# Transposes of three more tiles moved from TensorE to DMA in a chunked-attention and gated-FFN kernel, with later loads, other planned landing times and 12 load buffers

## The chip, the cores and the metric

The kernel runs on one core of a Trainium2 chip. The metric is the device time of one execution in microseconds (us). Three runs of the kernel before gave 244.65, 244.76 and 244.78 us.

## What is computed

An attention over chunks of 32 rows is followed by a gated feed-forward network (FFN). There are 4 batches, 8 heads, 768 rows and a head dimension of 64; each chunk sees 16 rows to its left, itself, 8 rows to its right, and 8 memory rows of its head.

```
for c in range(nc):                       # 24 chunks of 32 rows, batch and head by batch and head
    k_full = concat(mem_k, k[c*32-16 : c*32+40]);  v_full likewise
    a = softmax(q[c] @ k_full.T / 8);     out[c] = a @ v_full
x = out, as 3072 rows of 512
y = (maximum(x @ w_gate, 0) * (x @ w_val)) @ w_out      # 512 -> 1536 -> 512
```

Inputs and output are float32 in HBM; inside, the matmuls run on 16-bit tiles.

## The kernel before

The 3072 rows are 24 tiles of 128, six to a batch (tiles 0 to 5 are batch 0, 6 to 11 batch 1, 12 to 17 batch 2, 18 to 23 batch 3). The FFN works on blocks of tiles: `BLOCKS = [2, 2, 2, 4, 4, 4, 4, 2]`, so block 3 is tiles 6 to 9, block 4 tiles 10 to 13, block 5 tiles 14 to 17.

*A tile's attention.* q and k come in as `qk_b` (a load by POOL's queue that casts to bf16, line 254) and are transposed to `qT` and `kT`; `scores` (line 309) writes S to PSUM; DVE and ACT make the softmax `p_n` (lines 322 to 352); P is transposed to `pT`; `values` (line 388, or 374 and 381 in batch 0) multiplies by `v_bd`, and `x_copy` puts the result, already transposed, into the block's `xT`. The scores of a tile need the k of the next tile of its batch too. `v_bd` holds v of one batch in the layout that the values need; there are two of them, used in turn, so batch 2's v goes where batch 0's was (after the values of tile 5 and after zeroing, lines 134 and 136), and batch 3's where batch 1's was (after the values of tile 11). v comes by four loads of POOL (line 185) and eight copies of the memory rows (line 168); `upper` (from line 190) shifts rows inside it.

*Two ways to transpose.* For tiles below `LATE_QK` (q, k) and `LATE_P` (P), PE does it: four 128x128 products with an identity (line 275 for q and k, 358 for P; 236 in batch 0), and ACT or DVE copies the result out of PSUM. For tiles from that number on, a transposing DMA from SP's queue does it (line 283 for q and k, line 362 for P). q and P land where they are used; k lands in `k_t` (three buffers) and is copied into `kT` by DVE or ACT.

*A block's FFN.* For each of 12 column groups, `first` (line 407) makes `g_ps` and `v_ps` with four matmuls each, ACT applies the relu (line 413), DVE multiplies (line 419); then `second` (line 432) makes the outputs, which ACT copies and sends out from its own queue (line 439).

*What sets the order.* Nothing is ordered by hand. Each piece of work is an `op` with its engine, an assumed duration, the work that it depends on, a priority and the buffers that it takes and gives. `schedule()` (line 682) walks through assumed time and, on each engine, starts the ready op of best priority: attention has priority 1, FFN 2, so that FFN fills PE between the attention's steps. A dependency may carry a lag, as `(("t", a, 0), LAND)`: the transfer counts as landed that long after its issue. On PE, after an assumed 36 us, attention ops also wait for a `MARGIN` of 1.0 us. The order so found is the order of instructions in each engine's queue; at run time each queue goes strictly in that order and waits for what its next instruction really needs. POOL's loads go in the order of the list built from line 639 on: `late` is k and q of tiles 6 to 23, in that order (k, q, k, q), and slices of it are put behind each batch's v (line 674).

*Holding back.* `pace(a)` keeps PE's transposes of tile a from being planned before the FFN has reached a point that lies `LEAD` = 31 us of assumed FFN time ahead of the tile's block, plus `STEP` = 5.2 us per tile within the block. It is used only for tiles that PE transposes. `pace_t(a)` keeps the transposing transfers of tile a behind the scores of tile a - 6.

## Time and profile before

| | |
|---|---|
| median of three runs | 244.76 us |
| the profiled execution's own time | 244.74 us |
| its span in the trace | 242.7 us |
| PE busy, matmuls | 235.8 us, 2706 |
| DVE, ACT, POOL busy | 147.9, 136.0, 77.9 us |
| granted TensorE clock | 0.998 |
| bytes by DMA, mean rate | 25.17 MB, 104 GB/s |
| transposing transfers of SP | 9 of k, 9 of q, 9 of P |

The page cuts the span into 40 slices of about 6 us and gives each engine's busy share in tenths. Instructions are named by line: L407 is line 407. A row of the chain has a start, a length and what ran; it goes from the last instruction back to whatever released each step. A row of a timeline has a start, a length, the engine, the line, the operation, the tile written and the tile read, and in brackets the idle time before it. SPq and POOLq are the queues from which DMAs are issued. A queue's row gives packets, MB, and the time of its packets as a share of 16 engines; several packets can be in flight on one engine, so a share may pass 100%. q0 carries POOL's loads, q1 SP's transfers, q10 the outputs.

Landmarks, from PE's timeline: scores of tile 12 at 101.35 us, of 13 at 109.90, of 14 at 126.17; values of tile 11 at 105.51, of 12 at 111.02, of 13 at 118.12, of 14 at 136.84, of 17 at 150.63, of 18 at 154.60; first matmul of block 3 at 85.66, of block 4 at 122.40, of block 5 at 160.12. POOL's last loads for tile 23 are issued at 122.45.

### The profile page before, as it was taken

The page shows a single profiled execution, that of the slowest core. Times are in us where ns is not written, and L with a number is a line of the kernel's source. Part 1 is how long each engine was busy: PE and PEld are TensorE (multiplying, and loading weights), DVE is VectorE, ACT ScalarE, POOL GpSimd, SP SyncE. Part 2 cuts the span into 40 slices and gives each one's busy share as a digit, 9 for nine tenths or more (in the row PEclk, how much of TensorE's full clock was granted, in tenths as well). Part 3 has the DMA queues.
Part 4 walks back from the last instruction along what each step waited for, and adds up shares of the span by engine and source line. Part 5 has one row for each costly group of instructions (what it writes and reads, how often), then busy time and mean ns, then how long its engine had stood idle before and what let it go on. Part 6 is the DMA issues. An engine that isn't in the chain of part 4 may idle for free.

```text
span 242.7 us, 6546 instructions
## 1 busy us (share of the span) xinstructions
PE 235.8 (97%) x2706; PEld 140.8 (58%) x2706; DVE 147.9 (61%) x296; ACT 136.0 (56%) x288; POOL 77.9 (32%) x102
## 2 busy tenths in 40 slices
PE   7898999999999999999999999999999999999994
PEld 5587887884589545554544545554445444445873
DVE  6674876988877458977549999894431043410430
ACT  7477777767885499665756674453332233312432
POOL 8975689235984396037430000000000000000000
PEclk9999999999999999999999999999999999999999
DMA  6999999999999999999990142651001210012102
GB/s 72 172 179 203 201 164 172 193 131 134 191 195 154 80 168 136 120 124 153 116 218 7 36 53 48 131 133 24 0 0 46 86 43 0 3 43 86 43 3 86
DMA packets 96413, 25.17 MB, mean 104 GB/s; under 512 B 87424, under 2 KB 93312, under 8 KB 96384
## 3 DMA queue, kind: packets, MB, share of 16 engines
q0 software_dynamic: 76128, 14.65, 83.5%
q1 hardware_dynamic: 16656, 3.82, 15.0%
q10 hardware_dynamic: 3600, 6.29, 8.1%
q8 instruction: 21, 0.34, 0.7%
q14 instruction: 8, 0.07, 0.1%
HBM read 28.55 MB, written 6.29 MB: 144 GB/s over the span
## 4 chain that ended last, share of the span: by engine, by line
PE 88%; ACT 4%; DMA 2%; POOL 2%; DVE 2%; issue 1%; ACTq 0%; POOLq 0%
PE v_ps L407 26%; PE g_ps L407 25%; PE out_ps L432 22%; PE xT_ps L388 3%; DMA v_n<-in_v_dram 2%; PE s_ps L309 2%; PE idle_ps L141 2%; PE vs_ps L215 2%; PE xT_ps L381 2%; PE pT_ps L358 2%; ACT v_bd L79 1%; PE qk_ps L275 1%; PE qk_ps L236 1%; POOL qk_p L227 1%; ACT o_sb L79 1%
## 5 line engine op out<-in xcount | busy, mean ns | idle before, releaser
L419 DVE TENSOR_TENSOR gvT<-v_ps,g_relu 128x256 f16<-128x256 f32 (+1 forms) x96 | 52.9, 554 | 58.2 <-PE v_ps L407 43.2
L407 PE MATMUL v_ps<-xT,w_val_sb 128*128 128x256 f16 (+1 forms) x384 | 78.2, 326 | 0.1
L407 PE MATMUL g_ps<-xT,w_gate_sb 128*128 128x256 f16 (+1 forms) x384 | 78.2, 326 | 0.0
L413 ACT ACTIVATE g_relu<-g_ps 128x256 f16<-128x256 f32 (+1 forms) x96 | 47.0, 491 | 47.6 <-PE g_ps L407 45.9
L432 PE MATMUL out_ps<-w_out_sb,gvT 128*128 128x512 f16 (+2 forms) x300 | 65.3, 371 | 0.0
L407 PEld LDWEIGHTS <-w_gate_sb 128*128 128x128 f16 x384 | 36.3, 98 | 23.1
L407 PEld LDWEIGHTS <-w_val_sb 128*128 128x128 f16 x384 | 36.0, 98 | 22.3 <-issue 0.5
L432 PEld LDWEIGHTS <-gvT 128*128 128x128 f16 x300 | 27.9, 98 | 29.9
L79 ACT COPY o_sb<-out_ps 128x512 f32<-128x512 f32 (+2 forms) x25 | 14.2, 567 | 31.8 <-PE out_ps L432 25.6
L337 ACT ACTIVATE p_exp<-dif 128x256 f16<-128x256 f32 (+2 forms) x72 | 19.6, 340 | 4.4 <-DVE dif L329 3.5
L322 DVE TENSOR_REDUCE mx<-s_ps 128x8 f32<-128x512 f32 x24 | 16.5, 688 | 5.6 <-PE s_ps L309 5.4
L341 DVE TENSOR_REDUCE sm<-p_exp 128x8 f32<-128x512 f16 x24 | 16.4, 683 | 4.4 <-ACT p_exp L337 4.1
L254 POOL DMA_DIRECT2D qk_b<-in_q_dram x18 | 16.4, 912 | 7.4 <-DMA v_bd<-in_v_dram 5.5
L254 POOL DMA_DIRECT2D qk_b<-in_k_dram x18 | 16.2, 903 | 5.5 <-DMA w_out_sb<-in_moe_w_out_dram 4.4
L79 ACT COPY v_bd<-v_bd 24x768 f16<-24x768 f16 (+1 forms) x20 | 15.6, 818 | 2.2 <-ACT o_sb L79 1.2
L352 DVE TENSOR_TENSOR p_n<-p_exp,rinv 128x512 f16<-128x512 f16 x24 | 16.5, 687 | 0.4
L329 DVE TENSOR_TENSOR dif<-s_ps,mx 128x512 f32<-128x512 f32 x24 | 16.4, 682 | 0.2
L185 POOL DMA_DIRECT2D v_bd<-in_v_dram x12 | 10.9, 920 | 12.5 <-PE v_ps L407 11.8
L168 POOL DMA_DIRECT2D v_bd<-vmem x16 | 10.5, 661 | 12.5 <-DMA v_bd<-in_v_dram 10.5
L79 ACT CAST xT<-xT_ps 128x512 f16<-128x512 f32 x17 | 9.9, 583 | 6.2 <-PE xT_ps L388 4.8
L141 PE MATMUL idle_ps<-idle 128*128 128x256 bf16 x69 | 11.5, 319 | 1.1 <-DVE warm L475 1.1
L388 PEld LDWEIGHTS <-v_bd 128*128 128x128 f16 x288 | 9.7, 96 | 3.2 <-issue 0.2
(57 smaller groups left out, 179.5 us busy)
## 6 DMA issues: line engine op xcount, KB each, us to landing
out_dram<-o_sb ACTq DMA_DIRECT2D x23, 256.0 KB
qk_b<-in_k_dram POOLq DMA_DIRECT2D x18, 128.0 KB, 7.2
qk_b<-in_q_dram POOLq DMA_DIRECT2D x18, 128.0 KB, 7.0
v_bd<-in_v_dram POOLq DMA_DIRECT2D x6, 384.0 KB, 11.5
w_out_sb<-in_moe_w_out_dram POOLq DMA_DIRECT2D x2, 768.0 KB, 10.5
qk_p<-in_k_dram POOLq DMA_DIRECT2D x3, 256.0 KB, 5.7
qk_p<-in_q_dram POOLq DMA_DIRECT2D x3, 256.0 KB, 6.6
v_n<-in_v_dram POOLq DMA_DIRECT2D x6, 128.0 KB, 6.5
```

What stands on the lines that cost most here:

```text
L79: nc.scalar.copy(o, i)
L254: nc.gpsimd.dma_start(qk_b[a, i], bass.AP(tensor=x.tensor, offset=x[b, 0, 128 * t, 0].offset, ap=[[D, 128], [S * D, H], [1, D]]))
L322: nc.vector.reduce_max(SM[a, "mx"], s4, axis=AX.X)
L329: nc.vector.tensor_tensor(out=SM[a, "dif"].rearrange("p (m r) a s -> p r m a s", r=2), in0=S_ps.pop(a).rearrange("p r (m a) s -> p r m a s ...
L337: nc.scalar.activation(p[:, :, :, s0:s0 + k1 - k0], dif[:, :, :, k0:k1], ACT.Exp, scale=SCALE)
L341: nc.vector.reduce_sum(SM[a, "sm"], SM[a, "p"], axis=AX.X)
L352: nc.vector.tensor_tensor(out=P_n[a], in0=SM.pop((a, "p")), in1=rinv_b, op=ALU.mult)
L388: nc.tensor.matmul(ps[:, hp, r], lhsT=v_bd[b % NSET][:, hp, 4 * t + g, :], rhs=x[:, hp, r], start=True, stop=True)
L407: nc.tensor.matmul(ps, lhsT=w[:, f, 128 * m:128 * m + 128], rhs=xTs[blk][:, f, :], start=(f == 0), stop=(f == NFC - 1))
L413: nc.scalar.activation(st["r", m], st.pop((0, m)), ACT.Relu)
L419: nc.vector.tensor_tensor(out=st["gv"][:, m, :], in0=st.pop((1, m)), in1=st.pop(("r", m)), op=ALU.mult)
L432: nc.tensor.matmul(st["o", t, c], lhsT=st["gv"][:, m, 128 * t:128 * t + 128], rhs=w_out_sb[:, m, c[0]:c[1]], start=(m == 0), stop=(m == ND ...
```

## The change

- `LATE_QK` and `LATE_P` go from 15 to 12: tiles 12, 13 and 14 are transposed by DMA too.
- The load buffers (`ldpool`) go from 18 to 12.
- Behind batch 1's v, POOL loads `late[5:12]` (8's q to 11's q) where it loaded `late[5:21]` (up to 16's k); behind batch 2's v, `late[12:33]` (12's k to 22's k) where it loaded `late[21:33]`; behind batch 3's v the same three loads as before.
- Tiles 10 and 11, the only ones of block 4 that PE still transposes, are paced by 44 in place of `LEAD` = 31. A transposing transfer is held behind the scores of tile a - 4, not a - 6.
- The assumed landing times become tables by tile: q and k 7.5 us for tiles below 14, 18.0 for 16 to 20, 10.0 for the rest (4.5 for all before); P 8.5 below 14, 18.0 for 14 and 15, 13.0 from 16 on (3.0 for all before). The assumed issue time is 1.5 us (1.4 before), and what a transposing transfer adds to the assumed DMA queue is 1.5 us (1.1 before).
- The planner looks at more points in time: at each lag that a user of the finished op has, with and without the margin.

```diff
-    LATE_QK, LATE_P = 15, 15
+    LATE_QK, LATE_P = 12, 12
-    ldpool = ctx.enter_context(tc.tile_pool(name="ldpool", bufs=18))
+    ldpool = ctx.enter_context(tc.tile_pool(name="ldpool", bufs=12))
-            "qk": 18, "xT": 2, "gv": 2, "gr": 3, "o": 3, "kv": 2}
+            "qk": 12, "xT": 2, "gv": 2, "gr": 3, "o": 3, "kv": 2}
-        at = begun[blk] - LEAD + STEP * (a - starts[blk]) - (AHEAD if a >= LATE_P else 0.0)
+        at = begun[blk] - (44 if blk >= 4 else LEAD) + STEP * (a - starts[blk]) - (AHEAD if a >= LATE_P else 0.0)
-    ISSUE, LAND, SLACK, LAND_P = 1.4, 4.5, 1.0, 3.0
+    ISSUE, SLACK = 1.5, 1.0
+    LAND = {a: 7.5 if a < 14 else 18.0 if 16 <= a < 21 else 10.0 for a in range(NT)}
+    LAND_P = {a: 8.5 if a < 14 else 18.0 if a < 16 else 13.0 for a in range(NT)}
     def pace_t(a):
-        return [("s", a - 6)]
+        return [("s", a - 4)]
-            op(("pc", a), {"SP": ISSUE}, ..., [("pn", LAND_P)])
+            op(("pc", a), {"SP": ISSUE}, ..., [("pn", min(LAND_P[a], 7.0))])
-        for a, i in late[5 if b == 1 else 9 + 12 * (b - 1):21 + 12 * (b - 1)]:
+        for a, i in late[(5, 12, 33)[b - 1]:(12, 33, 36)[b - 1]]:
             load_qk_op(a, i)
-                            queue_end += 1.1 if e == "SP" and key[0] in ("t", "pc") else ...
+                            queue_end += 1.5 if e == "SP" and key[0] in ("t", "pc") else ...
-                    for x in (end, done[key], done[key] + 0.2, done[key] + 1.5, done[key] + MARGIN):
+                    lags = {d[1] for k in users.get(key, ()) for d in ops[k]["deps"] if timed(d) and d[0] == key}
+                    for x in [end] + [done[key] + lag + m for lag in lags | {0.0, 0.2, 1.5} for m in (0.0, MARGIN)]:
```

In the other places `LAND` and `LAND_P` become `LAND[a]` and `LAND_P[a]`.

More of the change, by code (lines that the diff above doesn't have):

```diff
@@ L534 @@
                    [(("qk", a, i), SLACK), ("new", b)],
-                   (1, a - i, 0), ["kt"] if i else [], [("qk", LAND)], pace_t(a))
+                   (1, a - i, 0), ["kt"] if i else [], [("qk", LAND[a])], pace_t(a))
                 if i:
                     op(("tc", a, i), {"DVE": (0.2, 0.29), "ACT": (0.52, 0.62)}, lambda e, a=a, i=i: qk_copy(a, i, engine[e]),
-                       [(("t", a, i), LAND)], (1, a - i, 0), (), ["kt"])
+                       [(("t", a, i), LAND[a])], (1, a - i, 0), (), ["kt"])
                 continue
@@ L544 @@
         op(("s", a), {"PE": 0.36}, lambda e, a=a: scores(a),
-           [(("t", a, 0), LAND) if a >= LATE_QK else ("tc", a, 0), ("tc", a, 1)]
+           [(("t", a, 0), LAND[a]) if a >= LATE_QK else ("tc", a, 0), ("tc", a, 1)]
            + ([] if last else [("tc", a + 1, 1)] if b or t % 2 == 0 else [("tc", a + 1, 1), ("tc", a + 2, 1)])
@@ L560 @@
         else:
-            op(("pc", a), {"SP": ISSUE}, lambda e, a=a: p_transfer(a), [("nrm", a)], (0, a), ["pT"], [("pn", LAND_P)])
+            op(("pc", a), {"SP": ISSUE}, lambda e, a=a: p_transfer(a), [("nrm", a)], (0, a), ["pT"], [("pn", min(LAND_P[a], 7.0))])
         if b == 0:
@@ L572 @@
         op(("v", a), {"PE": 0.45 if b else 1.0}, lambda e, a=a: values(a),
-           [("pc", a) if a < LATE_P else (("pc", a), LAND_P)]
+           [("pc", a) if a < LATE_P else (("pc", a), LAND_P[a])]
            + ([("vl", b, n) for n in range(2)] + [("up", b, n, m) for n in range(2 * HP) for m in range(t // UT + 1)]
@@ L769, in schedule @@
                         if queue_end > t:
-                            queue_end += 1.1 if e == "SP" and key[0] in ("t", "pc") else 0.7 if key[0] == "oc" else 0.0
+                            queue_end += 1.5 if e == "SP" and key[0] in ("t", "pc") else 0.7 if key[0] == "oc" else 0.0
                         fn = lambda o=o, e=e: o["fn"](e)
```

## The prediction

> **What bounds the kernel now.** I read the page's first two parts, then the waits of TensorE, then the chain from 98 us on.

> ```profile
> span 242.7 us, 6546 instructions
> PE 235.8 (97%) x2706; PEld 140.8 (58%) x2706; DVE 147.9 (61%) x296; ACT 136.0 (56%) x288; POOL 77.9 (32%) x102
> PE   7898999999999999999999999999999999999994
> ```

> TensorE (PE) is busy in every slice from the second on; the 6.9 us that it lacks lie mostly before 23 us (3.2) and after 239 us (3.1). In 100 to 123 us it is busy 23.00 of 23.00 us, at a granted clock of 1.00. No wait of PE for a transfer is listed after the start. So a microsecond of PE work that goes is a microsecond of time, as long as no wait of PE replaces it. The chain shows what a PE transpose costs there:

> ```profile
> 98.85 0.45 PE qk_ps L275 x8
> ...
> 105.45 0.22 PE qk_ps L275 x4
> ...
> 106.93 0.22 PE qk_ps L275 x4
> ...
> 108.88 0.22 PE pT_ps L358 x4
> ...
> 118.67 3.90 PE out_ps L432 x18
> 122.57 0.86 PE g_ps L407 x4
> ```

> Four transposes take 0.22 us of the path, and the matmuls behind them keep their usual 0.86 us. Block 4 (tiles 10 to 13) begins at 122.57; tile 13's values ended at 118.67, so in this stretch attention is 3.9 us ahead of its use.

> **What goes from PE.** Tiles 12, 13 and 14 lose q, k and P on PE: nine groups of four. In the chain these are half of the 0.45 at 92.66 (12's k), the 0.45 at 98.85 (12's q, 13's k), 0.22 at 105.45, 106.93 and 123.43 (13's q, 14's k and q), and P at 108.88, 116.11 and 134.19 (0.22, 0.22, 0.23). Sum: 0.23 + 0.45 + 3 x 0.22 + 0.67 = **2.0 us**. With them go nine copies out of PSUM (0.41 to 0.66 us on DVE or ACT); three copies of the transposed k come (0.28 on DVE, 0.62 on ACT). I cost these at nothing: PE, not they, ends last, and in 123 to 160 us DVE was busy 32.64 of 37 us while PE lost only 0.14. If PE's cover were gone, DVE and ACT would be relieved by some 3 us together (nine times about 0.5, less 1.4), a gain.

> **What comes: nine more transposing transfers.** Each is an instruction on SP, 1.19 to 2.69 us there. SP's queue is otherwise waiting, so that is free unless one waits for its data: then the transfers behind it wait too, P included. On the DMA engines one alone, in 136 to 139 us, is 544 packets:

> ```profile
> q1 hardware_dynamic: 544, 0.13, 21.7%
> ```

> It was issued at 136.57 and its packets ran from about 137.6 to 138.6: two microseconds, of which one is data. Nine are some 9 us of DMA time. Before has room: POOL waits 11.8 us until 107.0 for tile 11's values before it may issue batch 3's v, and nothing moves from 129 to 137. I take 0.

> Beside loads a transfer is slower. Here are SP's rows, then the queues in 72 to 76 and in 76 to 84 us:

> ```profile
> 71.98 1.31 SPq L283 DMA_TRANSPOSE k_t<-qk_b  x1
> 73.50 1.93 SPq L283 DMA_TRANSPOSE qT<-qk_b  x1
> 75.52 1.22 SPq L283 DMA_TRANSPOSE k_t<-qk_b  x1
> ```
> ```profile
> q0 software_dynamic: 4111, 0.52, 208.1%
> ```
> ```profile
> q0 software_dynamic: 2056, 0.39, 86.4%
> q1 hardware_dynamic: 1632, 0.39, 66.7%
> ```

> In the first stretch no packet of q1 (SP's queue) moved, although a transfer had been issued at its start; in the second 1632 = 3 x 544 moved. Counting them microsecond by microsecond, the three end at about 78.4, 80.5 and 83.8: 6.4, 7.0 and 8.3 us after issue. The twelve transfers issued from 88.63 to 115.85, counted in the same way (544 each, in order of issue), took 3.8 to 8.2 us. So these rows bound a landing between 2 us (alone) and 8.3 us.

> [...]

> **What moves: loads and their use.** In before, POOL issues 11's q at 57.87 and then nine loads (12's k to 16's k) ahead of batch 2's v:

> ```profile
> 66.00 0.94 POOL L254 DMA_DIRECT2D qk_b<-in_k_dram  x1
> 67.46 3.80 POOL L185 DMA_DIRECT2D v_bd<-in_v_dram  x4 [0.52 <-DVE p_n L352]
> ```

> With those nine behind, v can be issued at about 58.7 (the zeros that it needs were done at 55.6). It and its eight row copies took 67.46 to 84.26 in before, with seven loads in front and three transposes beside them; with less of both I estimate 12 us, so 12's k is issued at about 71 and lands near 76 (16's q, in that position, was issued at 84.26 and transposed at 88.63, 4.4 us later). Its transposes then land at 82 to 85, 13's k at about 87, and tile 12's scores can run some 12 us before their 101.35 of before. Tiles 10 and 11 are let go 13 us of planned block time earlier (44 for 31), so they need not hold it up. Block 4 has its x with over 10 us to spare; I cost the move at 0. The bounds: -0.4 (the 0.25 us at 69.10 and 0.12 at 144.54 that PE lost in before) and, if a landing is late, the stall of the first rival.

> With 12 load buffers instead of 18, 18's k takes 12's k buffer and 22's k takes 16's k, and POOL's later loads stand behind them, batch 3's v too. What waits for that is tile 18's values, at 154.6 in before, against v landed by 119: 35 us of cover, so 0; above that, microsecond for microsecond. Block 5's tiles had their values at 150.63, its first matmul ran at 160.12: 9 us of cover.

> What is planned decides where PE *waits*, since its queue is in order: a score placed before its transfer has landed holds every matmul behind it. The planner now counts 7.5 us to landing for tiles 12 and 13 (10 for 14, 15; 18 for 16 to 20; 8.5 for P of 12 and 13), and after 36 us it adds a margin of 1.0 for PE's attention work. 7.5 + 1.0 = 8.5 is above the largest landing counted, 8.3. In before nothing tested this: 15's k was copied at 93.28, 15 us after it landed.

> **Sum.** The profiled execution took 244.74 (span 242.7 and 2.0 around it), the median 244.76; the two are the same within 0.1. 244.74 - 2.0 = **242.7 us**, 0.8% less.

> **Rivals.**

> *Late landing (slower).* PE stands at tile 12's or 13's scores or values for transfers that land after their planned time. For it: these are the first transposed tiles that PE needs soon after their transfer, and the row copies of batch 2's v, in the same stretch of DMA, landed only 11.5 us after issue (median of three, 72 to 76 us). A q or k as late as these costs 11.5 - 8.5 = 3.0 us, P as late costs 11.5 - 9.5 = 2.0; both 5.0: 244.74 - 2.0 + 3.0 = 245.7, with both 247.7. It decides from 2.0 us of stall in all. Against it: no counted landing reached 8.5, and a stall delays PE's later work, so later transfers have more time: it is paid once or twice, not per tile. A load of tile 12 that lands later than planned has the same price. Chance 0.24.

> *Stall as large as the gain (no change).* 1.5 to 2.5 us of the same, or of DVE: tiles from 14 on are no longer held back (14's q was at 123.27 in before) and bunch where DVE is already busy 8.2 of 10 us (100 to 110); one gate product late holds a PSUM buffer. In 130 to 140 DVE was busy 9.5 of 10 and PE lost nothing, which speaks against it. 244.2 to 245.3. Chance 0.14.

> *The transposing queue becomes the bound.* If transfers beside loads were served one by one, each for its whole 7 us, tile 13's x would stand behind nine of them (q and k of 12 and 13, k of 14, q of 14, k of 15, two P): from 76 to 139, and block 4, due at about 121, would begin 18 us late: about 261. Speaking against: twelve landed between 94 and 122, 2.5 us apart. Chance 0.02. [...]

> *As forecast*, stalls under 1.5 us: 242.2 to 244.2, chance 0.60. That the transposes do not leave PE is excluded by the code.

> **Numbers.** A measurement of this kernel can tell about 0.2% (0.49 us). Faster 0.60; within it 0.14; slower 0.24 + 0.02 = 0.26. The range, 242.1 to 246.5: it leaves out some 0.04 below, and above it the part of late landing with both prices (0.12) and the third rival (0.02).

> **What would show it.** Right: PE's matmuls down by 36 (24 at line 275, 12 at 358), PE busy down by about 2 us, no wait of PE for k_t, qT or pT, SP with 36 transposes. Wrong: an idle row of PE or its weight loads before line 309 or 388 between 85 and 125 us, with a transfer as releaser; a block 4 that begins after 122.6; or a full PE whose busy time did not fall.

## The result and the profile after

The changed kernel took 243.33 us (median of 20 runs, 242.82 to 247.72) beside 244.62 us (244.31 to 245.20) for the kernel before: ratio 0.9952, 95% interval 0.9937 to 0.9967, 0.5% faster where 0.8% was forecast. The first profiled execution, at 247.72 us, is left out of that ratio; it is read below because it holds the wait of the first rival. A second profile, of an execution near the median, is the one to set beside the kernel before. Its page begins:

```profile
span 241.3 us, 6483 instructions
PE 234.0 (97%) x2670; PEld 138.6 (57%) x2670; DVE 149.0 (62%) x295; ACT 135.4 (56%) x283; POOL 77.2 (32%) x102
```

36 matmuls and 1.8 us of PE busy time are gone, 1.4 us of span. Summed from each group's start to the next start in PE's timeline, line 275 fell from 4.03 to 2.68 us and line 358 from 3.91 to 3.21: 2.05 us by these rounded rows, 2.0 by the instructions' own times. Two stretches show where the rest went. From block 2's first matmul to the first of the last outputs: 167.27 us before (66.93 to 234.20), 165.42 now (67.00 to 232.42), 1.85 less. From there to the end of the span: 8.50 before, 8.88 now, 0.38 more. Between 85 and 126 us, where the first rival has PE stand, it does not; this is the chain of that profile around tile 14's scores:

```profile
104.22 0.86 PE v_ps L407 x4
105.09 0.24 PE s_ps L309 x32
105.33 0.97 PE g_ps L407 x4
```

PE does lose something earlier, in block 2 (PE's timeline of the same profile):

```profile
75.54 0.60 PE L407 MATMUL v_ps<-xT,w_val_sb 128*128 128x256 f16 x4
75.97 0.60 PE L407 MATMUL g_ps<-xT,w_gate_sb 128*128 128x256 f16 x4
76.80 0.60 PE L407 MATMUL v_ps<-xT,w_val_sb 128*128 128x256 f16 x4 [0.23 <-ACT g_relu L413]
```

Such a group of four has 0.44 us to the next; here it is 0.83, and 0.12 was lost a microsecond before: 0.5 us. ACT was copying shifted rows of batch 2's v (0.83 us each) while the relus waited, as its timeline shows:

```profile
75.51 0.83 ACT L79 COPY v_bd<-v_bd 24x768 f16<-24x768 f16 x1
76.37 0.66 ACT L413 ACTIVATE g_relu<-g_ps 128x256 f16<-128x256 f32 x2
```

In the kernel before nothing is lost there.

**The execution at 247.72 us.** The same instructions, PE's timeline:

```profile
105.19 0.22 PE L309 MATMUL s_ps<-kT,qT 64*32 64x64 bf16 x6
108.18 0.39 PE L309 MATMUL s_ps<-kT,qT 64*32 64x64 bf16 x26 [2.77 <-DVE kT L81]
108.50 1.89 PE L407 MATMUL g_ps<-xT,w_gate_sb 128*128 128x512 f16 x4
110.19 1.58 PE L407 MATMUL v_ps<-xT,w_val_sb 128*128 128x512 f16 x4
111.60 1.03 PE L407 MATMUL g_ps<-xT,w_gate_sb 128*128 128x512 f16 x4
```

Tile 14's scores need the k of tile 15; its transfer is the first step of the chain there:

```profile
98.86 8.95 DMA k_t<-qk_b
107.81 0.02 issue
107.83 0.30 DVE kT L81
```

This transfer was late at its issue more than on its way. It landed 8.95 us after issue, within the 10 us that the planner counts for tile 15; PE came to the scores that need it at 105.41, only 6.5 us after the issue. Its data were there: by the trace's semaphore records the load of 15's k had landed at 88.54. In the same records SP's and ACT's DMAs, 73 in this execution and 64 in the kernel before, take eight semaphores in turn, and none was issued before the last DMA that had its semaphore had landed: the shortest time between the two is 0.06 us here and 7.1 us in the kernel before. So SP's queue stood twice for stores of outputs (SP's waits in this execution):

```profile
SPq L283 <- DMA out_dram<-o_sb: 7.5, 2, 5.0
```

The second of these stores was issued at 89.55 and landed at 98.72, just ahead of the issue of 15's k at 98.86. For the kernel before no such wait is listed. In the ordinary execution (experiment 1) the two waits take 7.7 us; there 15's k was issued at 97.26 and its copy ended at 104.60, only 0.4 us before tile 14's scores. No run here takes these waits away.

PE stood 2.77 us, and the next eight matmuls took 3.1 us in place of 1.7. The busy times by stretch show why (the number before the last two is the granted clock):

```profile
106.00:108.00 2.00, 0.00 (x0) 0.00 (x0) 0.17 (x1) 0.00 (x0) 0.00 (x0) 0.97 2.84 53
108.00:110.00 2.00, 1.82 (x30) 0.82 (x30) 1.97 (x5) 0.00 (x0) 1.32 (x2) 0.50 2.01 174
110.00:112.00 2.00, 2.00 (x7) 0.75 (x6) 1.97 (x5) 0.60 (x1) 1.95 (x3) 0.68 2.72 135
```

The granted clock was 0.50 from 107.89 to 111.30 us, the last 3.1 us of it behind the wait, so a wait of 2.8 us cost some 4.2 of the 4.6 us by which this span is longer. POOL's timeline bounds the landings in this execution, since a load waits for the transfer that still reads its buffer:

```profile
92.95 0.87 POOL L254 DMA_DIRECT2D qk_b<-in_k_dram  x1 [2.16 <-DMA k_t<-qk_b]
97.00 0.87 POOL L254 DMA_DIRECT2D qk_b<-in_q_dram  x1 [3.17 <-DMA qT<-qk_b]
98.42 0.87 POOL L254 DMA_DIRECT2D qk_b<-in_k_dram  x1 [0.55 <-DMA k_t<-qk_b]
```

These are 13's k, 13's q and 14's k, issued at 83.39, 85.09 and 86.43: at most 9.6, 11.9 and 12.0 us to landing. The load goes some 0.5 us behind the landing: 15's k landed at 107.81, and the load that waited for it went at 108.34.

### The profile page after: what moved, and what is told of

Read it like the earlier page. It is cut to its first block, busy times and chain, and to the rows that moved or that the text cites. A ratio compares the mean times of both kernels' runs of the same rounds, so it can differ in the third digit from the quotient of the medians.

```text
span 245.9 us, 6483 instructions
## 1 busy us (share of the span) xinstructions
PE 235.4 (96%) x2670; PEld 138.7 (56%) x2670; DVE 148.5 (60%) x295; ACT 135.2 (55%) x283; POOL 77.5 (32%) x102
## 4 chain that ended last, share of the span: by engine, by line
PE 81%; DMA 11%; issue 2%; POOL 2%; ACT 1%; DVE 1%; ACTq 0%; DVEq 0%; POOLq 0%
PE out_ps L432 23%; PE g_ps L407 23%; PE v_ps L407 23%; DMA v_bd<-in_v_dram 4%; DMA k_t<-qk_b 4%; PE xT_ps L388 2%; DMA v_n<-in_v_dram 2%; PE s_ps L309 2%; PE idle_ps L141 2%; PE vs_ps L215 2%; PE xT_ps L381 1%; DMA v_bd<-vmem 1%; PE pT_ps L358 1%; PE qk_ps L236 1%; POOL qk_p L227 1%
## 5 line engine op out<-in xcount | busy, mean ns | idle before, releaser
L407 PE MATMUL v_ps<-xT,w_val_sb 128*128 128x256 f16 (+1 forms) x384 | 78.7, 328 | 0.4 <-ACT g_relu L413 0.2
L407 PE MATMUL g_ps<-xT,w_gate_sb 128*128 128x256 f16 (+1 forms) x384 | 79.0, 329 | 0.0
L432 PE MATMUL out_ps<-w_out_sb,gvT 128*128 128x512 f16 (+2 forms) x300 | 65.4, 371 | 0.0
L407 PEld LDWEIGHTS <-w_val_sb 128*128 128x128 f16 x384 | 36.3, 98 | 24.7 <-issue 2.0
L407 PEld LDWEIGHTS <-w_gate_sb 128*128 128x128 f16 x384 | 36.4, 98 | 23.8 <-issue 0.7
L432 PEld LDWEIGHTS <-gvT 128*128 128x128 f16 x300 | 28.0, 98 | 30.4
L254 POOL DMA_DIRECT2D qk_b<-in_q_dram x18 | 16.4, 913 | 19.0 <-DMA qT<-qk_b 6.1
L79 ACT COPY v_bd<-v_bd 24x768 f16<-24x768 f16 (+1 forms) x25 | 20.0, 819 | 1.6 <-ACT o_sb L79 1.2
L254 POOL DMA_DIRECT2D qk_b<-in_k_dram x18 | 16.5, 914 | 11.4 <-PE pT_ps L358 3.9
L352 DVE TENSOR_TENSOR p_n<-p_exp,rinv 128x512 f16<-128x512 f16 x24 | 16.5, 687 | 0.5
L185 POOL DMA_DIRECT2D v_bd<-in_v_dram x12 | 10.9, 922 | 0.1
L79 ACT CAST xT<-xT_ps 128x512 f16<-128x512 f32 x13 | 7.6, 585 | 5.8 <-PE xT_ps L388 4.6
## 6 DMA issues: line engine op xcount, KB each, us to landing
v_bd<-in_v_dram POOLq DMA_DIRECT2D x6, 384.0 KB, 12.4
```

Of the source, the lines that this page charges most:

```text
L79: nc.scalar.copy(o, i)
L254: nc.gpsimd.dma_start(qk_b[a, i], bass.AP(tensor=x.tensor, offset=x[b, 0, 128 * t, 0].offset, ap=[[D, 128], [S * D, H], [1, D]]))
L352: nc.vector.tensor_tensor(out=P_n[a], in0=SM.pop((a, "p")), in1=rinv_b, op=ALU.mult)
L407: nc.tensor.matmul(ps, lhsT=w[:, f, 128 * m:128 * m + 128], rhs=xTs[blk][:, f, :], start=(f == 0), stop=(f == NFC - 1))
L432: nc.tensor.matmul(st["o", t, c], lhsT=st["gv"][:, m, 128 * t:128 * t + 128], rhs=w_out_sb[:, m, c[0]:c[1]], start=(m == 0), stop=(m == ND ...
```

## The experiments

Times are medians beside runs of the kernel before in the same sessions (244.45 to 244.67 us).

**1. The changed kernel again** (no edit).

> The changed kernel once more, for a profile beside the 245.9 us span that was profiled first. Theory (2.0 us of PE work go, and what is missing from 2.0 is PE standing at a score whose transposed k landed late): 242.7 to 243.5 us, 1.2 to 1.9 us below the kernel before; the profile shows one or two idle rows of PE before line 309 between 85 and 125 us, 0.3 to 1.0 us in all, each released by the copy of k_t. Rival (the nine groups of transposes cost PE less than 2.0 us, and nothing waits): the same time, but no idle row of PE there.

243.22 us, ratio 0.9949 (0.9936 to 0.9962). No wait of PE between 85 and 125 us: the theory of experiment 1 falls for an ordinary execution, and its rival's premise (a group is cheap) falls in experiment 2. This is the second profile above.

**2. The nine groups twice.**

```diff
-        for hp in range(HP):
+        for hp in [hp for _ in range(2 if 12 <= a < 15 else 1) for hp in range(HP)]:   # in qk_t and in p_t
```

> The kernel before, with the PE transposes of q, k and P of tiles 12, 13 and 14 each done twice (36 products more, the second overwriting the first with the same values), in an otherwise unchanged order. Theory (nine groups at 0.22 us on a PE that ends last): 2.0 us more than before, 246.6 to 246.8. Rival (a group costs less because PE's time beside it is partly idle): 0.5 to 1.3 us more.

246.60 us, ratio 1.0085 (1.0073 to 1.0097): 1.9 us more, as priced. The groups are worth 1.9 us of time, in this kernel, at this place.

**3. More time planned to landing.**

```diff
-    LAND = {a: 7.5 if a < 14 else 18.0 if 16 <= a < 21 else 10.0 for a in range(NT)}
+    LAND = {a: 14.0 if a < 16 else 18.0 if 16 <= a < 21 else 10.0 for a in range(NT)}
```

> The changed kernel, with 14 us counted to the landing of q and k of tiles 12 to 15 (7.5 and 10 in the change), so that PE's scores of these tiles come later in its queue. Theory (late landing is what is missing): no idle row of PE before line 309 between 85 and 125 us, 242.5 to 242.9 us, and the executions lie closer together than the changed kernel's. Rival (the gain was less than 2.0 for another reason): the same as the changed kernel, 243.0 to 243.5.

245.03 us (243.59 to 246.75), ratio 1.0014 (0.9993 to 1.0035): the whole gain is gone, and neither expectation holds. The scores of 12 to 15 move to 101 to 122 us, and the waits move on: PE stands 0.54 us at block 4's first matmul, at 122.73, for tile 13's x, 0.21 and 0.34 us at scores behind it. Later is not safer; it brings tile 13 up to block 4.

**4. Everything but the transposes.**

```diff
-    LATE_QK, LATE_P = 12, 12
+    LATE_QK, LATE_P = 15, 15
```

> The changed kernel with LATE_QK and LATE_P back at 15: loads behind batch 2's v, 12 buffers, the pacing and the landing table stay, PE transposes tiles 12, 13 and 14 as before. Theory (the gain is the PE work alone, the rest is worth nothing): 244.4 to 245.0 us, as the kernel before. Rival (the new order of loads or the finer planning is worth something by itself): outside 244.3 to 245.2, on either side.

245.25 us, ratio 1.0024 (1.0014 to 1.0034): the rest of the change by itself *costs* 0.6 us. The 0.5 us at 75 to 77 us are there (PE waits 0.23 us for the relu at 77.28), and block 2 to the last outputs takes 167.73 us, 0.46 more than before; the tail is 8.44. The transposes then gave 2.3 us in that stretch (167.73 to 165.42).

**5. Pacing 31 for tiles 10 and 11.**

```diff
-(44 if blk >= 4 else LEAD)
+LEAD
```

> The changed kernel, with the pacing of tiles 10 and 11 back at LEAD = 31 in place of 44. In the second profile of the changed kernel PE loses 0.5 us at 75 to 77 us, in block 2, to a relu of ACT that came late while tile 10's softmax ran; in the kernel before, tile 10 came at 86.5. Theory (the earlier tiles 10 and 11 cost what was missing from the 2.0 us): no loss at 75 to 77, 242.6 to 242.9 us. Rival (tile 12 then comes later or closer to tiles 10 and 11, and PE loses as much elsewhere): 243.2 us or more.

253.30 us, ratio 1.0352 (1.0318 to 1.0386). Of the 0.5 us at 75 to 77, 0.2 are left, and 10 us are lost instead. The chain of this kernel:

```profile
112.83 0.91 SPq L283
113.74 0.04 issue
113.79 15.67 DMA pT<-p_n
129.46 0.04 issue
129.50 0.60 PE xT_ps L388 x16
```

PE stood 8.27 us at tile 13's values; their P landed 15.67 us after issue, where the planner counts 8.5. POOL had issued batch 3's v just before:

```profile
107.64 3.65 POOL L185 DMA_DIRECT2D v_bd<-in_v_dram  x4
```

With 44, tile 13's P is issued at 108.39 and v at 108.40 (experiment 1's profile), and its values run at 117.8 with no wait.

**6. Seven small loads more.** They fill a spare tile at the start and compute nothing. SP and ACT issue 64 DMAs in the kernel before, 73 in the changed kernel and 80 here, so the last store has the eighth semaphore, the first, and the eighth again.

```diff
+        for j in range(7):
+            nc.sync.dma_start(spare[:, 16 * j:16 * j + 16], <the first 16 numbers of mem_k>)
```

> The changed kernel, with seven loads of 64 bytes more on SP's queue in the first microseconds, into a tile that nothing uses. SP's and ACT's DMAs take eight semaphores in turn; the kernel before has 64 such DMAs, the changed kernel 73, so its last store has the first semaphore, not the eighth; with 80 it has the eighth again. In the profiles the span ends 8.9 us after the first matmul of the last outputs in the changed kernel, 8.5 in the kernel before. Theory (SP checks the semaphores in order at the end, and a last store on the first of them leaves the other checks behind it): the tail is 8.4 to 8.5 us, and the time falls by 0.3 to 0.5 against the changed kernel's 243.2. Rival (the longer tail has to do with the transposes or with where the last store lands): tail 8.8 to 9.0 and 243.1 to 243.4 us.

242.91 us (242.25 to 245.40), ratio 0.9948 (0.9924 to 0.9972). The tail is 8.47 us: the page of this kernel and its last outputs in PE's timeline are

```profile
span 241.1 us, 6492 instructions
```
```profile
232.63 5.37 PE L436 MATMUL out_ps<-w_out_sb,gvT 128*128 128x512 f16 x36
```

against 241.3 and 232.42 without. So the 0.4 us of tail follow from the number of SP's and ACT's DMAs, not from what they carry; the six kernels here with the last store on the eighth semaphore have 8.4 to 8.5, those with it on the first 8.9 to 9.0. SP's instructions in the traces show why: at the end SP waits on the eight semaphores one after another, 0.06 us each. In experiment 1 the last store's is the first, and the eight waits run from 240.02 to 240.44 (from 244.62 to 245.05 in the execution at 247.72 us); in the kernel before only that of the last store is left when it lands, at 241.78. By the medians it is worth 0.3 us; the two intervals overlap.

**7. The transposes alone.**

```diff
 # kernel before
-    LATE_QK, LATE_P = 15, 15
+    LATE_QK, LATE_P = 12, 12
```

> The kernel before with LATE_QK and LATE_P at 12 and nothing else: the transposes move, the order of loads, 18 buffers, pacing and the landing times of 4.5 and 3.0 us stay. Theory (planned landing times below the real ones make PE stand): PE waits for k_t or pT several times between 85 and 160 us, in all 2 us or more, and the 2.0 us are lost: 244.7 to 250. Rival (the transposes alone do it): 242.4 to 243.0 us.

251.96 us, ratio 1.0316 (1.0279 to 1.0353). The theory holds and was too mild. PE's waits:

```profile
PE xT_ps L388 <- DMA pT<-p_n: 6.5, 5, 3.0
```

Five waits for P, planned 3.0 us after issue; one of these transfers was issued at 114.06 and landed 10.70 us later.

**8. The old landing times in the new order.**

```diff
+    LAND = {a: 4.5 for a in range(NT)}
+    LAND_P = {a: 3.0 for a in range(NT)}
```

> The changed kernel with the landing times of the kernel before, 4.5 us for q and k and 3.0 for P, for all tiles. Theory (the new order of loads needs the new landing times): PE waits for transposing transfers, 2 us or more in all, 245 to 250 us. Rival (the scores come late enough behind the loads anyway): 242.8 to 243.5 us.

254.87 us, ratio 1.0408 (1.0386 to 1.0430). PE's waits:

```profile
PE xT_ps L388 <- DMA pT<-p_n: 4.7, 2, 3.9
PE s_ps L309 <- ACT kT L79: 1.8, 1, 1.8
```

**9 and 10. Batch 3's v behind tile 13's values**, with pacing 31, and with pacing 44 and the seven loads.

```diff
-([("v", TPB * (b - NSET + 1) - 1)] if b > NSET else [])
+([("v", TPB * (b - NSET + 1) + 1)] if b > NSET else [])
```

> The changed kernel with pacing 31 for tiles 10 and 11, as in the run that took 253.3 us, and batch 3's v held back until tile 13's values have been issued (tile 11's before). In that run PE stood 8.3 us at tile 13's values: its P was sent to transpose at 113.8 us, 6 us after batch 3's v was issued, and landed at 129.5. Theory (a transposing transfer behind batch 3's v lands 10 to 16 us after issue, and that alone makes the 10 us): no wait of PE over 2 us for pT of tiles 12 and 13, and 242.5 to 246 us. Rival (the transfers are late among themselves, or behind the loads of q and k): 250 us or more, with PE at tile 12's or 13's values again.

> The changed kernel with the seven small loads (last store on the eighth semaphore) and batch 3's v behind tile 13's values. Theory (P of tiles 12 and 13 then has only loads of q and k beside it, and what is left of lateness goes): 242.2 to 242.9 us, with executions closer together than the 242.25 to 245.4 of the seven small loads alone. Rival (holding v back moves its collision to P of tiles 14 and 15, which the planner gives 18 us): the same 242.9, or above it.

254.88 us, ratio 1.0411 (1.0380 to 1.0442), and 242.86 us (242.60 to 243.06), ratio 0.9928 (0.9913 to 0.9944). Neither tests what it was made for: the edit changes only what the planner assumes, and POOL's queue has nothing of tile 13 to wait for at run time, so v was issued at 107.68 and 108.34, as in 5 and 1. In 9 tile 13's P again landed late (issued 113.23, 17.95 us). That batch 3's v makes the transfers late rests on their order in time, in 5, 7 and 9; it was not isolated.

**11. Pacing 40, with the seven loads.**

```diff
-(44 if blk >= 4 else LEAD)
+(40 if blk >= 4 else LEAD)
```

> The changed kernel with the seven small loads and pacing 40 in place of 44 for tiles 10 and 11. Theory (at 44 tile 10's softmax falls into block 2, where PE loses 0.5 us at 75 to 77; at 31 tile 13's P falls behind batch 3's v; between them neither need be paid): 242.3 to 242.8 us. Rival (tile 13 is already as late as it may be): above 243.5 us, with a wait of PE for pT.

242.72 us (242.37 to 242.93), ratio 0.9924 (0.9908 to 0.9939), the fastest here: 1.7 us below the kernel before, 0.6 below the changed kernel, with intervals that touch. The relu's wait at 76.8 is gone and no wait for pT came; block 2 to the last outputs takes 165.42 us as with 44, so what is better against the changed kernel is the tail, 8.50. What was won in block 2 is lost again: PE stands 0.25 us at 69.05, as in the kernel before, and tile 14's scores take 0.54 us in place of 0.31, for the copy of 15's k that ended at 104.77:

```profile
104.58 0.54 PE L313 MATMUL s_ps<-kT,qT 64*32 64x64 bf16 x32
```

**12. 18 load buffers.**

```diff
-tc.tile_pool(name="ldpool", bufs=12)      and "qk": 12
+tc.tile_pool(name="ldpool", bufs=18)      and "qk": 18
```

> The changed kernel with 18 load buffers in place of 12. POOL waits 15 us for buffers that transposing transfers still read in the changed kernel. Theory (buffers are off the path, batch 3's v is not needed for 35 us): 243.0 to 243.5 us, as the changed kernel. Rival (12 buffers hold loads back that would otherwise crowd the transposes of tiles 12 and 13, so 18 make those land later): above 244.5 us, with a wait of PE for kT or pT.

245.28 us (243.92 to 251.17), ratio 1.0041 (1.0011 to 1.0070): the gain is gone. With 18, batch 3's v goes out at 99.3 us, 9 us earlier than with 12, ahead of tile 12's and 13's P (101.65 and 107.58). The profile is of the fastest of these executions (243.92) and shows no wait of PE for a transfer; that the slower ones had one is the likely reading of their spread, but none was recorded.

## Why the prediction was right, and where it was wrong

- *What bounds the kernel, and 2.0 us of PE work.* Right: 2.0 us in the timeline, 1.9 us in experiment 2.
- *What comes, at 0.* Mis-sized by 0.38 us: nine more DMAs of SP turned the last store's semaphore from the eighth to the first, and the end of the program got longer. That was outside the sum altogether. And SP's queue was not otherwise free, as the step had it: its transfers stood 7.5 to 7.8 us for stores of outputs (the first profile, experiments 1 and 11). No wait of PE followed in the ordinary execution, but it is what made 15's k late in the other.
- *What moves, "I cost the move at 0".* Wrong in both directions. With tiles 10 and 11 pulled into block 2, PE loses 0.5 us there. The waits of 0.25 us at 69.10 and 0.12 at 144.54, the prediction's own lower bound, are gone in return, so the stretch is 1.85 us shorter and not 2.0. Nor is that 0.5 us simply to be had: with pacing 40 it is gone and the stretch is as long (experiment 11). Tile 12 came later than estimated, its k issued at 73.92 for 71 and its scores at 94.83 for some 89. And the move is what the gain stands on: without it 253.3 us (experiment 5). "They need not hold it up" was right; that without it all would collapse was not seen.
- *The landing between 2 and 8.3 us.* The bound was too low. I counted packets and assigned them in order of issue; in the execution at 247.72 us the same count gives 93.4 for 13's q, and the load that waited for it went at 97.0. Loads that waited for a transfer went 7.7 to 12.4 us after its issue there; in the ordinary execution those that waited for 14's k and q went 11.0 and 10.8 us after. P took 10.7 to 18.0 us in experiments 5, 7 and 9. So 7.5 + 1.0 was not above the largest landing, and that PE did not wait rests on the 10 us planned for tile 14 and on luck: 0.4 us were left.
- *12 buffers at 0, "35 us of cover".* Batch 3's v was indeed not missed. But 12 buffers are no neutral saving: with 18 the gain is gone (experiment 12). That the earlier v does it was not isolated.
- *Late landing, the rival.* It happens, though not as described: in the execution at 247.72 us PE stands at the scores of tile 14, not 12 or 13, and the transfer, which landed within its planned time, had been issued late behind a store. By the prediction's own signs, an idle row before line 309 with a transfer as releaser, that execution speaks for the rival. That the price of one wait (3.0 us) fits the 2.77 is luck, since it came from a landing 3.0 us later than planned; the halved clock behind it, 1.4 us, was not in it. In the ordinary execution it costs nothing.
- *Stall as large as the gain.* Not seen in the changed kernel; it is what experiment 3 turned into.
- *The transposing queue as the bound.* Not seen: 36 transfers fitted.

So the forecast 242.7 was 0.6 us low: 2.0 from PE, less 0.38 of tail, 0.15 by which the stretch fell short and 0.07 by which block 2 began later, gives the 1.4 us by which the span fell. Experiment 11, where the tail is back, is at 242.72; that this meets the forecast is in part luck, as it is 1.7 us below the kernel before in its session, not 2.0.

## What to carry to other kernels

Work taken from a full engine pays at its price only if nothing in that engine's in-order queue waits in its place, so the planned landing time of what replaces it belongs to the change as much as the move itself: here the same nine groups gave -1.3, +7.4 or +10.3 us (the changed kernel, experiments 7 and 8). A landing is read from whoever waited for it, not from the count of packets. And when the order of a whole queue is replanned, price the reordering by a run of its own (experiment 4): it was not free. A transfer can also be late because its issue was held: 15's k, in the execution at 247.72 us, went at 98.86, behind a store of ACT that had the same semaphore and landed at 98.72.
